# A mixed attention and soft-MoE kernel on one core: the first v load on another queue, and phi loaded in long rows

## The chip, the cores and the metric

One core of a Trainium2 chip runs the whole program. The metric is the device time of one execution in microseconds. Five engines work side by side: TensorE (PE in the profile, its weight loads as PEld), VectorE (DVE), ScalarE (ACT), GpSimd (POOL) and SyncE (SP). Each runs its own instructions in order and waits on semaphores for the others. Transfers are issued from an engine's queue and run on the core's 16 DMA engines.

## The reference, cut to what matters

The input is q, k, v (4 batches, 8 heads, 768 positions, 64 features, float32), a flag per head, and the MoE's phi (512 x 32), w1 (8 x 512 x 1024) and w2 (8 x 1024 x 512), all float32.

```
scores = q @ k.T / 8                       # per batch and head
keep   = causal                            # flagged heads
keep   = causal & (first 4 keys | the last 64 keys)   # the other heads
x      = softmax(scores where keep) @ v    # as (3072, 512): position by (head, feature)

logits = x @ phi                           # (3072, 32)
d      = softmax over the 3072 rows of logits
slots  = d.T @ x                           # 32 slots, 4 for each of 8 experts
slot_out[e] = relu(slots[e] @ w1[e]) @ w2[e]
c      = softmax over the 32 slots of logits
out    = c @ slot_out                      # (3072, 512) float32
```

## The kernel before

The work is cut into eight quads Q = 0..7, half a batch each (four heads), and sixteen pairs n of heads, two in a quad. For each quad, q, k and v are loaded as float32 and written to SBUF as bfloat16 by GpSimd's queue, 96 partitions by 2 x 1024, into one of two buffers for each of the three (`raws`, which lie in the memory of w2s[4], w2s[5] and w2s[6]; the masks `msk` lie in w2s[7]). TensorE turns each with 32 small products (`turn`, L120; in the order list Tq0.0, Tk0.0, Tv0.0 and so on), and VectorE or ScalarE copies the result out of PSUM (L130, L132). v is turned back into blocks (L138). Scores are made in units of 512 columns for two heads (`qk`, L166), exponentiated by ScalarE (L174), masked by VectorE (L193), multiplied with v (`pvmm`, L208) and normalised (L222). After each batch the rows of x are turned (L231) and multiplied with phi (L255), exponentiated over slots (L260) and put in output order by GpSimd (L264). After the last batch come the experts: w1 (L639), the turn of the hidden rows (L652), w2 (L666), and then the output products (L704, L720), evacuated by VectorE and ScalarE and stored by SP's queue (L690).

The order of all this on every engine is written out by hand in `ORDER`; each engine executes its part in that order. In it, Y means `zeros`: products of zeros that keep TensorE busy (L422). Eleven of them run at the very front, ahead of Tq0.

All loads of q, k, v and the weights are issued by GpSimd (L103, L391, L394, L397), in the order of `LOADS`. The first six (q0 k0 v0 q1 k1 v1) are issued at once. Each later one is issued, in that order, when the buffer that it goes to has been turned: q2 behind both halves of Tq0, k2 behind Tk0, v2 behind Tv0. The w entries take the weights in turn, w1 of expert 0 first. The last ones, w2 of experts 4 to 7, take the place of the raws and the masks and so come at the end, experts 6 and 7 in two column halves each.

phi is (512, 32). It is wanted in SBUF as 128 partitions by 4 chunks, the rows in the order of the heads in a pair's halves, and repeated four times along the columns. Before, SP's queue issues four loads into `phf`, each of 128 runs of 32 floats, once the second half of Tv1 has been issued:

```
nc.gpsimd.memset(phf[:, 0, 0:1], 0.0)      # L503: makes SP's queue wait for this point
for hp in range(2):
    for qh in range(2):
        nc.sync.dma_start(phf[64 * hp:64 * hp + 64, 2 * qh:2 * qh + 2, :], ...)   # L506
```

and GpSimd casts and repeats it into `phi` behind Tv2 (L510). The first use of phi is at L255, at 41 us. SP's queue issues besides only the head flags `ri` at the front (L409) and the stores at the end.

GpSimd's instructions at the front are, in order: the issue of q0, an iota (L412), the issues of k0, v0, q1, k1, v1, `perm` (L456), and the issues from q2 on, each with its wait. ScalarE's first ones are the load of its table, a one-column exponential, and the first half of kT (L130).

Of the kernel before, what the change touches and what calls it, by code (L numbers as in the profile page):

```python
# [10 lines left out]
F32 = mybir.dt.float32  # L11
# [24 lines left out]

LOADS = "q0 k0 v0 q1 k1 v1 q2 k2 v2 w q3 k3 v3 w q4 k4 v4 w q5 k5 v5 w q6 k6 v6 w q7 k7 v7 w".split()

ORDER = """
Tq0.0 Tq0.1 E eq0.0 eq0.1 Y4 Tk0.1 H2.3 H1.2 Tk0.0 H1.1 ek0.1A H0.1 H0.0 ek0.0 H0.2 H0.3 Y4 Q0.1 H1.3 Q0.4
# [34 lines left out]
class Attn:  # L77
# [19 lines left out]
        self.lg, self.el, self.ep, self.tp = {}, {}, {}, {}  # L97


    def load(self, t, Q):  # L100
        b, h0 = Q // 2, 4 * (Q % 2)
        s = self.src[t][b, h0:h0 + 4].rearrange("(hp hq) (r t) d -> (hq r) hp (t d)", hp=2, t=16)
        self.nc.gpsimd.dma_start(self.raws[t][Q % 2][:96], s)  # L103


    def blocked(self, t, Q):
# [223 lines left out]
def kernel(  # L330
# [13 lines left out]
    nc = tc.nc  # L344
    P = 128
    B, H, S, D = q.shape
    n_sink, window = int(n_sink), int(window)
    ES = moe_phi.shape[1]
# [8 lines left out]
    w2s = [singles.tile([P, 8, DM], BF16, name=f"w2_{e}") for e in range(NE)]  # L357
    raws = {}
    for i, t in enumerate("qkv"):
        w = w2s[4 + i].rearrange("p f (hp c) -> p (f hp c)", hp=2)  # L360
# [3 lines left out]
    ident = singles.tile([P, P], BF16, name="ident")  # L364
    phi = singles.tile([P, 4, P], BF16, name="phi")
# [23 lines left out]
    def w_load(i):  # L389
        if i < NE:  # L390
            nc.gpsimd.dma_start(w1s[i], moe_w1[i].rearrange("(di do) f -> di do f", do=4))  # L391
        else:
            e = i - NE
            nc.gpsimd.dma_start(w2s[e], moe_w2[e].rearrange("(fi fo) d -> fi fo d", fo=8))  # L394

    def w2_half(e, c):
        nc.gpsimd.dma_start(  # L397
            w2s[e][:, :, 256 * c:256 * (c + 1)],
            moe_w2[e].rearrange("(fi fo) d -> fi fo d", fo=8)[:, :, 256 * c:256 * (c + 1)])
# [5 lines left out]
    at = Attn(nc, tc, ctx, sctx, {"q": q, "k": k, "v": v}, env)  # L405


    ir32 = is_retrieval.tensor.reshape([H]).bitcast(I32)
    nc.sync.dma_start(ri, bass.AP(tensor=ir32, offset=0, ap=[[0, P], [1, 2 * H]]))  # L409
    iti = at.small.tile([P, P], I32, tag="iti", bufs=1, name="iti")  # L410
    at.load("q", 0)
    nc.gpsimd.iota(iti, pattern=[[1, P]], base=0, channel_multiplier=-1)  # L412
    for t in ("k0", "v0", "q1", "k1", "v1"):
        at.load(t[0], int(t[1]))

    zw = msk[:, H - 1, :]
    nc.vector.memset(zw, 0.0)
# [2 lines left out]
    def zeros(c):  # L420
        for i in range(c):
            nc.tensor.matmul(zp[:, i % 2, :], zw[:, :128], zw, start=True, stop=True)  # L422

    zeros(11)
    nc.vector.memset(quarter, 0.25)  # L425
    nc.vector.memset(zero, 0.0)
    nc.scalar.activation(colpart[:, 0:1], quarter, ACT.Exp)
# [23 lines left out]
    nc.vector.tensor_copy(fmask[:, :, 0], r0)  # L451


    nc.vector.tensor_scalar(marks[:, 0], r0, -1.0, 1.5, op0=ALU.mult, op1=ALU.add)
    nc.vector.tensor_scalar(marks[:, 1], r1, -1.0, 1.5, op0=ALU.mult, op1=ALU.add)
    nc.gpsimd.tensor_scalar(perm, iti, tkf[:, 2:3], None, op0=ALU.is_equal)  # L456
# [14 lines left out]
    def weights(c):  # L471
        for _ in range(min(c, 12 - wi[0])):
            w_load(wi[0])
            wi[0] += 1

    phf = at.small.tile([P, 4, ES], F32, tag="phf", bufs=1, name="phf")


    unread = []
# [6 lines left out]
        for i in range(c):  # L486
            nc.tensor.matmul(unread[0][:, 1, :448], ident, w1s[0][:, 0, :448], start=True, stop=True)

    queue = LOADS[6:]
    turns = {}  # L490

    def issue():

        while queue:
            x = queue[0]
            if x != "w" and turns.get((x[0], int(x[1]) - 2), 0) < 2:
                return
            queue.pop(0)
            weights(1) if x == "w" else at.load(x[0], int(x[1]))

    def load_phi():

        nc.gpsimd.memset(phf[:, 0, 0:1], 0.0)  # L503
        for hp in range(2):
            for qh in range(2):
                nc.sync.dma_start(phf[64 * hp:64 * hp + 64, 2 * qh:2 * qh + 2, :],  # L506
                                  moe_phi.rearrange("(qh hp a d) s -> qh hp d a s", qh=2, hp=2, a=2)[qh, hp])

    def copy_phi():
        nc.gpsimd.tensor_copy(phi.rearrange("p c (o s) -> p c o s", o=4),  # L510
                              phf.rearrange("p c (o s) -> p c o s", o=1).to_broadcast([P, 4, 4, ES]))

    def after_turn(t, Q):
        turns[t, Q] = turns.get((t, Q), 0) + 1
        issue()
        if (t, Q, turns[t, Q]) == ("v", 1, 2):
            load_phi()
        if (t, Q, turns[t, Q]) == ("v", 2, 2):
            copy_phi()
        if (t, Q, turns[t, Q]) == ("v", NQ - 2, 2):  # L520
            weights(12)
        if (t, Q, turns[t, Q]) == ("v", NQ - 1, 2):
            for e in (4, 5):
                w_load(NE + e)
            w2_half(6, 0)
# [3 lines left out]
    for name in ORDER:  # L529
        op, arg = name[0], name[1:].rstrip("A")  # L530
        eng = "ACT" if name[-1] == "A" else "DVE"
        a = arg.split(".")
# [13 lines left out]
        elif op == "N":  # L546
            at.norm(*[int(x) for x in a])
        elif op == "X":
            at.x_transpose(int(a[0]))
        elif op == "L":  # L550
            at.logits(int(a[0]), [int(c) for c in a[1]])
        elif op == "E":
            expert_masks()
        elif op == "S":
            at.exp_slots(int(arg))
        elif op == "B":
            at.slots_back(int(arg))
        elif op == "D":
            at.dispatch(int(arg))
        elif op == "Z":  # L560
            fill(int(arg))
        elif op == "Y":
            zeros(int(arg))
        elif op == "T":
            t, Q, h = arg[0], int(a[0][1:]), int(a[1])
            if t == "b":
                at.back(Q, h)
            else:
                at.turn(t, Q, h)
                after_turn(t, Q)  # L570
        elif arg[0] in "qkvb":
            t, Q, h = arg[0], int(a[0][1:]), int(a[1])
            (at.blocked_back if t == "b" else at.turned)(*(() if t == "b" else (t,)), Q, h, eng)
        else:
            {"X": at.x_transposed, "l": at.last_exps, "B": at.slots_turned, "D": at.dispatched}[arg[0]](int(arg[1:]))
# [197 lines left out]
```

## Time and profile before

| | |
|---|---|
| median of 3 runs | 152.35 us |
| the runs | 151.85, 152.35, 257.87 us |
| the profiled execution, whole | 152.03 us |
| its span | 150.3 us |
| busy: PE, DVE, ACT, POOL | 124.2, 113.4, 103.8, 35.0 us |
| moved by GpSimd's queue | 26.22 MB, counted as written |
| HBM read | 52.50 MB |

The span runs from the first to the last instruction of the profiled execution; the rest of its time lies around it. The page gives the busy time of each engine, the span in 40 slices of 3.76 us with a digit for the busy share in tenths, the share of the DMA engines and the GB/s that they moved, the chain of waits that ended last, and the costliest groups of instructions by line. A "releaser" is what ended an idle time. A load that changes float32 to bfloat16 is counted with the bytes that it writes.

### The profile page before, as it was taken

The numbers are of one execution on the slowest core, as the hardware profiler recorded it, in microseconds if no ns is written. First come the engines' busy times: TensorE is split into PE (matmuls) and PEld (weight loads), VectorE is DVE, ScalarE is ACT, GpSimd is POOL, SyncE is SP. The second block draws the span as 40 slices with busy tenths as digits, with TensorE's granted clock in tenths as the row PEclk, the third lists the DMA queues.
The fourth block names the chain that finished last, engine by engine and source line by source line (L and its number), as shares of the span: only waits on it lengthen the run. The fifth ranks groups of instructions, "written<-read, shape, count | busy, mean of one in ns | idle before, by whom it ended". The sixth has DMA issues, their size and how long they took to land.

```text
span 150.3 us, 5215 instructions
## 1 busy us (share of the span) xinstructions
PE 124.2 (83%) x2301; PEld 82.5 (55%) x2303; DVE 113.4 (75%) x257; ACT 103.8 (69%) x142; POOL 35.0 (23%) x68
## 2 busy tenths in 40 slices
PE   6799999999999999999999998987989923984000
PEld 2356677677667666658657766554764701651000
DVE  4998999999969999998999998899724301767000
ACT  3059899999899999889989987997054000788000
POOL 6724311411145021335800002800600000000000
PEclk9999999999999999999999999999999995699755
DMA  2999999999999999999999999999999999789995
GB/s 25 202 210 209 210 225 208 209 228 201 211 227 200 217 226 196 226 208 206 219 217 227 216 212 212 214 222 216 216 214 212 192 199 193 174 273 345 342 401 202
DMA packets 16838, 32.91 MB, mean 219 GB/s; under 512 B 1712, under 2 KB 9904, under 8 KB 15024
## 3 DMA queue, kind: packets, MB, share of 16 engines
q0 software_dynamic: 11168, 26.22, 91.0%
q1 hardware_dynamic: 5648, 6.37, 12.4%
q8 instruction: 18, 0.29, 0.7%
q14 instruction: 4, 0.03, 0.1%
HBM read 52.50 MB, written 6.29 MB: 391 GB/s over the span
## 4 chain that ended last, share of the span: by engine, by line
PE 32%; issue 20%; DMA 17%; ACT 13%; POOL 7%; DVE 2%; ACTq 0%; POOLq 0%
DMA w<-in_moe_w_dram 14%; PE sc L166 9%; PE pv L208 7%; ACT pT L174 7%; DMA w<-in_k_dram 4%; ACT ot L710 3%; PE tpv L120 3%; POOL expT L264 3%; PE tpk L120 2%; PE b L704 2%; PE tpx L231 2%; POOL w L394 2%; PE tpb L138 2%; PE lgs L255 1%; PE tpq L120 1%
## 5 line engine op out<-in xcount | busy, mean ns | idle before, releaser
L174 ACT ACTIVATE pT<-sc 128x1024 bf16<-128x1024 f32 (+1 forms) x96 | 81.1, 929 | 5.2 <-PE sc L166 4.9
L193 DVE TENSOR_TENSOR pT<-pT,w 128x1024 bf16<-128x1024 bf16 (+2 forms) x64 | 32.7, 527 | 2.6 <-ACT pT L174 2.5
L166 PE MATMUL sc<-qT,kT 64*128 64x512 bf16 (+3 forms) x256 | 32.5, 309 | 2.0 <-ACT pT L174 1.3
L208 PEld LDWEIGHTS <-pT 128*128 128x128 bf16 x672 | 25.0, 97 | 9.3 <-issue 7.2
L208 PE MATMUL pv<-vb,pT 128*128 128x65 bf16 x352 | 28.3, 194 | 0.1
L208 PE MATMUL pv<-vf,pT 128*128 128x65 bf16 x320 | 24.3, 194 | 0.0
L120 PEld LDWEIGHTS <-w 96*64 96x64 bf16 x768 | 18.6, 109 | 9.3 <-issue 6.2
L222 DVE TENSOR_TENSOR xb<-pv,rs 128x768 bf16<-128x768 f32 (+1 forms) x17 | 15.5, 910 | 0.6
L166 PEld LDWEIGHTS <-kT 64*128 64x128 bf16 x256 | 10.4, 93 | 9.8 <-issue 3.7
L710 ACT ACTIVATE ot<-b,rrow 128x256 f32<-128x256 f32 x16 | 6.3, 482 | 13.5 <-PE b L704 13.5
L264 POOL COPY expT<-ep 128x128 bf16<-128x128 bf16 x18 | 6.8, 426 | 21.8 <-ACT ep L260 21.8
L153 DVE TENSOR_TENSOR vf<-vb,fmask 128x528 bf16<-128x528 bf16 x16 | 11.2, 700 | 0.0
L666 PE MATMUL b<-w,hT 128*32 128x256 bf16 x128 | 5.7, 290 | 5.2 <-DMA w<-in_moe_w_dram 5.2
L103 POOL DMA_DIRECT2D w<-in_k_dram x8 | 5.1, 640 | 18.2 <-PE sc L166 12.0
L236 DVE COPY xT<-tpx 128x768 bf16<-128x768 bf16 x16 | 8.7, 551 | 0.7 <-PE tpx L231 0.7
L120 PE MATMUL tpq<-ident,w 96*64 96x96 bf16 x256 | 8.1, 209 | 0.8 <-DMA w<-in_q_dram 0.8
L231 PE MATMUL tpx<-ident,xb 128*128 128x128 bf16 x96 | 8.0, 218 | 1.0 <-DVE xb L222 0.8
L103 POOL DMA_DIRECT2D w<-in_q_dram x8 | 5.4, 670 | 13.3 <-PE tpq L120 12.4
L120 PE MATMUL tpk<-ident,w 96*64 96x96 bf16 x256 | 8.3, 208 | 0.2 <-DMA w<-in_k_dram 0.2
L120 PE MATMUL tpv<-ident,w 96*64 96x96 bf16 x256 | 8.3, 209 | 0.0
L132 DVE COPY qT<-tpq 128x768 bf16<-128x768 bf16 x15 | 8.0, 550 | 0.3 <-PE tpq L120 0.3
L422 PE MATMUL zp<-w 128*128 128x512 bf16 x21 | 7.0, 459 | 1.3 <-DVE quarter L425 1.2
(108 smaller groups left out, 153.4 us busy)
## 6 DMA issues: line engine op xcount, KB each, us to landing
w<-in_moe_w_dram POOLq DMA_DIRECT2D x14, 1024.0 KB, 18.9
out_dram<-ot SPq DMA_DIRECT2D x16, 256.0 KB, 3.2
w<-in_q_dram POOLq DMA_DIRECT2D x8, 384.0 KB, 12.5
w<-in_k_dram POOLq DMA_DIRECT2D x8, 384.0 KB, 10.9
w<-in_v_dram POOLq DMA_DIRECT2D x8, 384.0 KB, 11.0
w<-in_moe_w_dram POOLq DMA_DIRECT2D x4, 512.0 KB, 23.2
out_dram<-ot SPq DMA_DIRECT2D x4, 512.0 KB, 4.6
phf<-in_moe_phi_dram SPq DMA_DIRECT2D x4, 16.0 KB, 8.9
```

The source lines that it names most:

```text
L103: self.nc.gpsimd.dma_start(self.raws[t][Q % 2][:96], s)
L120: self.nc.tensor.transpose(tp[64 * hp:64 * hp + 64, x, :], raw[:96, hp, s * 64:s * 64 + 64], self.ident[:96, :96])
L153: self.nc.vector.tensor_mul(vf, self.vbs[n // 2 % 2][:, n % 2, :, :4, :], fm.to_broadcast([128, 2, 4, VW]))
L166: nc.tensor.matmul(sc[:, hh, o:o + w], kT[ps, (g0 + j) * 128:(g0 + j + 1) * 128], qT[ps, g0 * 128 + q0:g0 * 128 + q0 + w], start=True, sto ...
L174: self.nc.scalar.activation(self.pT[n][:, :, lo:hi], self.sc.pop((n, u))[:, :, :hi - lo], ACT.Exp, scale=self.scale)
L193: nc.vector.tensor_mul(v, v, m)
L208: self.nc.tensor.matmul(pv[:, i * 65:(i + 1) * 65], pT[:, hh, o:o + 128], (vb if i - j <= 1 else vf)[:, j, :65], start=(j == 0), stop=(j = ...
L222: nc.vector.tensor_mul(x[:, hs], pv[:, :, :, :64], rs[:, :c].to_broadcast([128, c, 6, 64]))
L231: self.nc.tensor.transpose(tp[:, i * 128:(i + 1) * 128], self.xb[b][:, i, n4 * 128:(n4 + 1) * 128], self.ident)
L236: self.nc.vector.tensor_copy(self.xT[n // 4][:, n % 4], self.tp.pop(("x", n, 0)))
L264: self.nc.gpsimd.tensor_copy(self.expT[:, b, t].rearrange("g (p s) -> g p s", s=16), self.ep[b][:, t].rearrange("g (s p) -> g p s", p=8))
L710: nc.scalar.activation(o[:, r, :], op[:, r, :], ACT.Copy, scale=rr[:, r:r + 1])
```

## The change

v0, the first load of v, is taken out of GpSimd's list. ScalarE's queue issues it as the program's first transfer, as float32, into memory that w2 of expert 3 takes later (`stage`). GpSimd casts it into its raw buffer after the issue of v1. phi is loaded by SP's queue right behind the head flags, each partition taking four rows of phi, 512 bytes, in one run. ScalarE casts it, TensorE turns it in four products (one for each of the four rows), ScalarE copies that out, and eight products with the identity put it in the order that the kernel wants; ScalarE copies and repeats it into `phi`. These products stand between the zeros at the front and Tq0: nine zeros, the four, two zeros, the eight. The loads, the memset and GpSimd's cast of before are gone.

```diff
-LOADS = "q0 k0 v0 q1 k1 v1 q2 k2 v2 w ...
+LOADS = "q0 k0 q1 k1 v1 q2 k2 v2 w ...
...
-    def load(self, t, Q):
+    def load(self, t, Q, queue=None, dst=None):
         b, h0 = Q // 2, 4 * (Q % 2)
         s = self.src[t][b, h0:h0 + 4].rearrange("(hp hq) (r t) d -> (hq r) hp (t d)", hp=2, t=16)
-        self.nc.gpsimd.dma_start(self.raws[t][Q % 2][:96], s)
+        d = self.raws[t][Q % 2] if dst is None else dst.rearrange("p (hp c) -> p hp c", hp=2)
+        (queue or self.nc.gpsimd).dma_start(d[:96], s)
...
     ir32 = is_retrieval.tensor.reshape([H]).bitcast(I32)
+    stage = w2s[3].rearrange("p f c -> p (f c)").bitcast(F32)
+    at.load("v", 0, nc.scalar, stage)
     nc.sync.dma_start(ri, bass.AP(tensor=ir32, offset=0, ap=[[0, P], [1, 2 * H]]))
     iti = at.small.tile([P, P], I32, tag="iti", bufs=1, name="iti")
+    phf = w2s[2][:, 0, :2 * 4 * ES].bitcast(F32)
+    nc.sync.dma_start(phf, moe_phi.rearrange("(p j) s -> p (j s)", j=4))
     at.load("q", 0)
     nc.gpsimd.iota(iti, pattern=[[1, P]], base=0, channel_multiplier=-1)
-    for t in ("k0", "v0", "q1", "k1", "v1"):
+    for t in ("k0", "q1", "k1", "v1"):
         at.load(t[0], int(t[1]))
+    nc.gpsimd.tensor_copy(raws["v"][0][:96].rearrange("p hp c -> p (hp c)"), stage[:96])
...
-    zeros(11)
+    zeros(9)
...
+    ph4 = w2s[2][:, 1, :4 * ES]
+    nc.scalar.copy(ph4, phf)
+    phr = at.scp.tile([ES, P, 4], F32, tag="sc", name="phr")
+    for j in range(4):
+        nc.tensor.matmul(phr[:, :, j], ph4[:, ES * j:ES * j + ES], ident, start=True, stop=True)
+    phT = w2s[2][:ES, 2, :]
+    nc.scalar.copy(phT, phr.rearrange("s p j -> s (p j)"))
+    zeros(2)
+    php = at.scp.tile([P, 4, ES], F32, tag="sc", name="php")
+    for n in range(4):
+        for hp in range(2):
+            h = 4 * (n // 2) + n % 2 + 2 * hp
+            nc.tensor.matmul(php[64 * hp:64 * hp + 64, n, :], phT[:, D * h:D * h + D], ident[:ES, :ES],
+                             start=True, stop=True)
+    nc.scalar.copy(phi.rearrange("p c (o s) -> p c o s", o=4),
+                   php.rearrange("p c (o s) -> p c o s", o=1).to_broadcast([P, 4, 4, ES]))
...
-    queue = LOADS[6:]
+    queue = LOADS[5:]
...
-    def load_phi():
-        nc.gpsimd.memset(phf[:, 0, 0:1], 0.0)
-        for hp in range(2):
-            for qh in range(2):
-                nc.sync.dma_start(phf[64 * hp:64 * hp + 64, 2 * qh:2 * qh + 2, :],
-                                  moe_phi.rearrange("(qh hp a d) s -> qh hp d a s", qh=2, hp=2, a=2)[qh, hp])
-    def copy_phi():
-        nc.gpsimd.tensor_copy(phi.rearrange("p c (o s) -> p c o s", o=4),
-                              phf.rearrange("p c (o s) -> p c o s", o=1).to_broadcast([P, 4, 4, ES]))
...
-        if (t, Q, turns[t, Q]) == ("v", 1, 2):
-            load_phi()
-        if (t, Q, turns[t, Q]) == ("v", 2, 2):
-            copy_phi()
```

More of the change, by code (lines that the diff above doesn't have):

```diff
@@ L35, in unit_pieces @@
     return out
-LOADS = "q0 k0 v0 q1 k1 v1 q2 k2 v2 w q3 k3 v3 w q4 k4 v4 w q5 k5 v5 w q6 k6 v6 w q7 k7 v7 w".split()
+LOADS = "q0 k0 q1 k1 v1 q2 k2 v2 w q3 k3 v3 w q4 k4 v4 w q5 k5 v5 w q6 k6 v6 w q7 k7 v7 w".split()
 ORDER = """
@@ L474, in weights @@
             wi[0] += 1
-    phf = at.small.tile([P, 4, ES], F32, tag="phf", bufs=1, name="phf")
     unread = []
```

## The prediction

> **What bounds the kernel now.** I read the page first, for the shape of the run, then the chain that ended last, then busy time by stage at the front and at the end, then the timeline around the waits.
>
> ```profile
> PEclk9999999999999999999999999999999995699755
> DMA  2999999999999999999999999999999999789995
> ...
> q0 software_dynamic: 11168, 26.22, 91.0%
> ```
>
> The DMA row is full from the second slice on: GpSimd's queue carries 26.22 MB (as written; the source is float32, twice that) at some 210 GB/s. The chain says how it ends:
>
> ```profile
> 105.35 20.53 DMA w<-in_moe_w_dram
> 125.88 0.04 issue
> 125.92 1.05 PE b L666 x11
> ```
>
> A w2 half is issued at 105.35 and lands 20.5 us later, behind everything issued before it. The stages show what the engines do meanwhile, and what the first microseconds look like (columns: window and its length, then busy us of PE, PEld, DVE, ACT, POOL, granted clock, DMA share, GB/s):
>
> ```profile
> 1.50:2.00 0.50, 0.50 (x2) 0.15 (x1) 0.00 (x0) 0.50 (x1) 0.50 (x1) 1.00 0.03 4
> 2.00:2.50 0.50, 0.50 (x3) 0.21 (x2) 0.05 (x1) 0.21 (x2) 0.41 (x3) 1.00 0.06 7
> 2.50:3.00 0.50, 0.50 (x3) 0.22 (x2) 0.47 (x5) 0.00 (x0) 0.50 (x1) 1.00 0.71 51
> 3.00:3.50 0.50, 0.50 (x3) 0.15 (x2) 0.43 (x3) 0.00 (x0) 0.50 (x2) 1.00 0.21 33
> 3.50:4.00 0.50, 0.50 (x2) 0.15 (x1) 0.46 (x3) 0.00 (x0) 0.50 (x2) 1.00 1.00 164
> ```
> ```profile
> 120.00:122.00 2.00, 0.59 (x20) 0.31 (x9) 0.00 (x0) 0.00 (x0) 0.00 (x0) 1.00 1.45 201
> 122.00:124.00 2.00, 0.38 (x2) 0.10 (x2) 0.00 (x0) 0.00 (x0) 0.00 (x0) 0.87 1.46 196
> 124.00:126.00 2.00, 0.08 (x4) 0.08 (x7) 0.00 (x0) 0.00 (x0) 0.00 (x0) 0.50 1.45 197
> ```
>
> So the end is set by a transfer stream that starts at 3.5 us and runs without a hole to about 129; all compute that can be done is done at 120.6, 5.3 us before the last first-half weights land. The stream's capacity before 3.5 us is nearly unused. An edit is worth what it does to the stream; a later front of the compute is free up to a point worked out below.
>
> ```profile
> 5.94 0.87 PE L120 MATMUL tpq<-ident,w 96*64 96x96 bf16 x32 [0.83 <-DMA w<-in_q_dram]
> 7.93 0.87 PE L120 MATMUL tpk<-ident,w 96*64 96x96 bf16 x32 [0.15 <-DMA w<-in_k_dram]
> ...
> 55.26 0.63 POOL L103 DMA_DIRECT2D w<-in_k_dram  x1 [8.05 <-PE sc L166]
> ...
> 123.43 0.38 PE L666 MATMUL b<-w,hT 128*32 128x256 bf16 x2 [2.84 <-DMA w<-in_moe_w_dram]
> ```
> ```profile
> w<-in_k_dram POOLq DMA_DIRECT2D x1, 384.0 KB, 6.9
> phf<-in_moe_phi_dram SPq DMA_DIRECT2D x4, 16.0 KB, 8.9
> ri<-in_is_retrieval_dram SPq DMA_DIRECT2D x1, 8.0 KB, 2.5
> ```
>
> **The change, part by part.** The sum is made against the profiled execution, 152.03 us (span 150.3, 1.73 around it); the median shown, 152.35, is 0.3 above it.
>
> *v0 leaves GpSimd's stream.* 393,216 bytes at 210 GB/s are 1.87 us less of it. On ScalarE's queue v0 is 786,432 bytes written as float32. The nearest row is the late float32 stores in 4 KB packets (403 GB/s from 144 to 148): 1.95 us. The issue can leave where SP's ri does, at 0.73, and ri's first packets show at 1.74. Free from there to 4.0, counting the stream's bytes against 210 GB/s, are 0.26+0.48+0.38+0.42+0.11 = 1.65 us, so 0.3 of v0 falls into the stream. Gain 1.87-0.3 = 1.6; lower bound 1.2 if the share column (0.71 at 2.5 to 3.0) is taken as occupied, upper 1.87.
>
> The Trainium skill (DMA: Bandwidth & Descriptors, section "Issuing engines are not separate DMA queues") says that DMAs from whatever engine run on the same 16 engines and interleave, so that a second issuing engine saves issue time only. By that rule moving v0 to another queue is worth nothing in itself; with the rows above it is worth the idle front alone, which is how I count it.
>
> *phi.* Four loads of 128 packets of 128 bytes ran from 23 to 31 us beside the stream; from 26 to 32 the queues together moved 216 GB/s, of which phi was some 11, so the stream had 205 instead of 214: 0.27 us lost over 6 us. Now it is one load of 128 packets of 512 bytes, 64 KB more in the crowded front, 0.15. Net gain 0.1 (0 to 0.27). GpSimd also loses a memset (0.13) and the phi cast (0.61, after 1.7 of waiting at 30 to 31.7); the next issue behind it waited for PE anyway, so nothing.
>
> Gain of the stream, G: 1.6 (1.1 to 2.1).
>
> *GpSimd's queue.* One issue fewer (0.65), so v1's issue ends at 4.9; then the cast of 96x2048, four times the phi cast's 128x512 (0.61): 2.4 us, to 7.3 if v0 has landed by 4.9. Behind it stand perm (0.69) and the issue of q2, which goes at 8.0 instead of 7.12, then k2. Cover: q2 landed 11.1 us after its issue against 4.6 for q0 on an empty stream, so 6.5 us of lateness cost nothing. The cast also has to be done by Tv0, at 10.24: 2.9 us of cover, after which PE would wait.
>
> *phi's chain stands ahead of Tq0 in PE's order.* Copy on ScalarE, four products, copy, eight products, and only then q0's turn. Cost after phi has landed: copy 128x128 about 0.3 (L285's 128x192 takes 0.33), four 128-wide products 0.4 (L295: six in 0.49), copy 32x512 0.69 (L644's 128x512), eight small products 0.3 (L248: 18 in 0.60), four handovers of 0.05: 1.9. The two zeros lie under the second copy, the broadcast copy into phi (0.7) under Tq0, before ScalarE's first kT copy.
> When does phi land? Lower: ri's packets end at about 3.05 and phi's 128 follow on the same queue at ri's pace (1.3 us): 4.3. Upper: the phf row, 7.9 to 9.9 us after issue, from 1.1: 9.0 to 11.0. From 25 to 30 us phi's packets alternated one for one with the stream's, 110 of each a microsecond; with v0 and q0 both in the way, twice that, so 128 take 1.2 to 2.4 us. I take 5.2. Tq0 then starts at 7.1 instead of 5.94. q0 itself, behind the last of v0, lands at about 6.4 and doesn't decide. With 0.2 for DVE beside the cast, the compute front is X = 1.4 us late (0 to 6).
>
> *Where X is paid.* Compute ends at 122.0 instead of 120.6, before the weights (125.9-1.6 = 124.3). But loads are issued when PE has freed a buffer, and the stream now runs 1.6 ahead of issues that come 1.4 later. The thinnest place is k6: issued at 55.26, landed 6.9 us on, against q0's 4.6 on an empty stream: 2.3 us of cover. Summing the stream's packets, the bytes ahead of k6 were moved at 59.6; less q0's 1.5 from issue to first packet the cover is 2.8. A hole of X+G less 2.55 = 0.5 us opens there.
>
> *End.* PE sat idle from 120.6 and its clock was granted at half from 123.5 to 130.3, so L666 took 1.04 us for 14 products (0.61 at 131.2, at full clock) and the 16 of L704 behind it 3.25 (1.91 at 132.4). With compute 1.4 later and weights 1.1 earlier PE waits from 122.0 to 124.8, with two products in between, about too short for that; stores begin a little earlier. 0.3, because the second half of the output waits for the last w2 half at 131.2 whatever PE does. Lower 0, upper 1.1: L666's 0.43 and half of L704's 1.34, the rest of which ScalarE's eight copies (3.3 us) hide.
>
> Sum: 152.03 - 1.6 - 0.3 + 0.5 = **150.6**.
>
> **The rivals.**
>
> *phi lands as late as it did (slower).* Speaking for it: phf's 7.9 to 9.9 us when the engines were full, and v0 fills them now. Against: ri, at the same early time, took 2.5. Landing at 9.0, Tq0 at 10.9, X = 5.0; PE idle from 4.4 to past 9 loses its clock as it did at 123.5, another 1.0. Hole 6.0+1.6-2.55 = 5.05: 152.03-1.6+5.05 = 155.5. It decides from X = 2.6, where hole and gain are equal.
>
> *Everything fits (faster).* v0 wholly in the idle front (1.87), phi's 0.27, no hole, and the 1.1 of a kept clock, with stores filling the 1.7 us in which the DMA engines idle between 128 and 133: 148.8. For it: PE may fall behind by less than 0.7. Against: at 131.2 PE waited for the last w2 half, so a faster first half of the output is only partly worth its time.
>
> *The pipe is the same.* If v0's packets take turns with q0's from the start, 1.95 us replace 1.87: 152.1. Against it, 1.65 us of idle engines. It is the rule of the Trainium skill named above (DMA: Bandwidth & Descriptors, same section) at its strictest.
>
> *The cast stops DVE.* A cast of 2.4 us beside DVE's work from 5 to 7.5 us, masks and qT copies, in the worst case adds all of itself to X: 3.8, hole 2.85, 153.0 with the end's 0.3. Against: beside phi's cast at 31.66 the DVE copy took 0.55 us, its mean. The Trainium skill (SBUF — State Buffer, section "Who interferes with whom") has GpSimd and some DVE modes exclude each other for a whole instruction; that DVE copy read PSUM, so no run here shows the case.
>
> **How the numbers follow.** Forecast 0.42, all fits 0.20, phi late 0.20, same pipe 0.10, cast 0.08. A measurement of this kernel can tell about 2%, 3 us. Below 149.0 lies the second case (0.20), above 155.1 the third (0.20), the rest within. The range leaves out half of the fast and half of the late case, 0.2: 148.8 to 155.5; the forecast's own is 149.6 to 151.6.
>
> **What would show it.** Right: stream share near 1 by 2.5 us; phi landing near 5; Tq0 at 6.5 to 7.5 behind the phi products; the w2 half that L666 waits for landing near 124.8; clock 1.0 between 123 and 130. Wrong: Tq0 past 8.5, a half clock before 12 us, a DMA share clearly under 1 around 55 to 62, or PE waiting for the cast at Tv0. If the weights land no earlier than 125.9 with no hole, the idle front was not room.

## The result

The changed kernel takes 156.56 us (median, 156.13 to 157.29) against 152.1: a ratio of 1.0304, 95% interval 1.0271 to 1.0337. It is slower, where 150.6 us was forecast. (The 152.1 is the median of four runs, one of which, a slow one, took 257.87 us; the ratios here and below leave slow runs out.) The profiled execution took 157.29 us with a span of 155.5, against 152.03 and 150.3 before: 5.2 us of span to explain.

The page of the changed kernel, the rows and the queue that were shown of before (q10 is ScalarE's queue, with v0 on it):

```profile
PEclk9999999999999999999999999999999999599855
DMA  1999999999999999499999999999999999989996
...
q0 software_dynamic: 10960, 25.82, 87.5%
q10 hardware_dynamic: 208, 0.79, 1.9%
```

GpSimd's queue has v0's 0.39 MB less to move, as intended. But the DMA row, full before, has a dip to 4 in its 17th slice (62 to 66 us). The windows show that hole and a thinner stretch at 18, and the front (columns as before: window, its length, busy us of PE, PEld, DVE, ACT, POOL, clock, DMA share, GB/s), and the same two later windows of the kernel before:

```profile
2.50:3.00 0.50, 0.50 (x3) 0.22 (x2) 0.47 (x5) 0.16 (x1) 0.50 (x2) 1.00 0.39 26
3.00:3.50 0.50, 0.50 (x3) 0.16 (x2) 0.43 (x3) 0.00 (x0) 0.50 (x2) 1.00 0.32 45
3.50:4.00 0.50, 0.50 (x2) 0.15 (x1) 0.46 (x3) 0.00 (x0) 0.50 (x2) 1.00 0.44 102
...
18.00:20.00 2.00, 2.00 (x48) 1.23 (x48) 2.00 (x9) 2.00 (x3) 0.53 (x1) 1.00 0.96 146
62.00:64.00 2.00, 2.00 (x40) 1.38 (x38) 2.00 (x4) 2.00 (x4) 0.96 (x2) 1.00 0.25 49
```
```profile
18.00:20.00 2.00, 2.00 (x45) 1.52 (x41) 1.91 (x5) 1.62 (x4) 1.30 (x3) 1.00 1.14 216
62.00:64.00 2.00, 2.00 (x43) 1.30 (x40) 1.97 (x6) 1.68 (x4) 1.27 (x2) 1.00 1.18 236
```

From 3.5 to 4.0 the share was 1.00 at 164 GB/s; now it is 0.44 at 102, and nearly all the bytes are v0's (12 packets of 4 KB; the other 28 are of under 512 bytes, on SP's queue). GpSimd's stream, which began at 2.8, moves its first packet at 6.1. The DMA issues, with KB each and us from issue to landing, show what that did to the four loads of the front:

```profile
w<-in_v_dram ACTq DMA_DIRECT2D x1, 768.0 KB, 8.3
...
w<-in_q_dram POOLq DMA_DIRECT2D x1, 384.0 KB, 9.5
...
w<-in_moe_phi_dram SPq DMA_DIRECT2D x1, 64.0 KB, 8.1
ri<-in_is_retrieval_dram SPq DMA_DIRECT2D x1, 8.0 KB, 5.3
```

ri took 2.5 us before, q0 4.6. The timeline says what came of it:

```profile
9.07 1.88 POOL L420 CAST w<-w 96x2048 bf16<-96x2048 f32 x1 [4.17 <-DMA w<-in_v_dram]
...
9.62 1.04 PE L464 MATMUL phr<-ident,w 128*32 128x128 bf16 x4 [4.42 <-ACT w L461]
...
11.87 1.49 PE L121 MATMUL tpq<-ident,w 96*64 96x96 bf16 x32
...
63.04 0.63 POOL L104 DMA_DIRECT2D w<-in_k_dram  x1 [8.06 <-PE sc L167]
...
132.08 0.67 PE L673 MATMUL b<-w,hT 128*32 128x256 bf16 x14 [2.27 <-DMA w<-in_moe_w_dram]
```

Tq0 starts at 11.87, 5.9 us later than before; its 32 products take 1.49 us instead of 0.87. PE had been idle for 4.4 us ahead of phi's products; in late_front below, where PE is kept busy, Tq0 starts almost as late and takes 0.87. By the attention's last exponential (112.2 instead of 104.4) the lateness is 7.8. k6 is issued at 63.04, 7.8 later too, and the last first-half weights let PE go at 132.08 instead of 125.92.

The best view is not one of the profile's. I summed the packets of GpSimd's queue in order of their times until each load's bytes were through, which tells about when its last byte moved. Before, in us, and then the difference from it (v0, which is off the queue in some, is left out of their sums):

```
load   before   after  v0_only  v0_half   v0_sp  v0_later  phi_only  late_front
q0       5.48   +3.48    +3.26    +0.99   +2.54     +0.14     +0.24       +0.07
q1      11.13   +1.57    +1.36    +0.04   +0.64     -0.52     +0.23       +0.06
q2      16.86   +2.15    +1.30    +0.01   +0.51     +4.61     +0.21       +0.02
v2      20.98   +3.11    +1.89    -0.02   +0.57     +4.67     +0.18       +0.77
k5      50.78   +2.95    +2.14    -0.05   +0.55     +4.63     -0.05       +0.97
q6      59.54   +3.82    +3.73    -0.04   +1.16     +5.24     -0.04       +2.22
k6      61.41   +5.81    +4.00    +0.06   +2.09     +7.74     -0.03       +3.31
w2     123.49   +6.28    +4.49    +0.07   +2.69     +8.33     -0.01       +3.77
last   130.91   +6.11    +4.03    +0.13   +2.33     +7.84     -0.13       +3.10
```

The column "after" has the whole story in four steps. The stream is held 3.48 us at the front. It gets 1.9 back where v0 would have been (between q0 and q1): 1.57 is left. Gaps from 18 to 22 add 1.5, and the hole at k6 adds 3.3 from k5 to the w2 half that PE waits for. Of 6.1 at the last load the span shows 5.2; 0.9 comes back at the end.

### The profile page after: what moved, and what is told of

Read it like the earlier page. It is cut to its first block, busy times and chain, and to the rows that moved or that the text cites. A ratio compares the mean times of both kernels' runs of the same rounds, so it can differ in the third digit from the quotient of the medians.

```text
span 155.5 us, 5235 instructions
## 1 busy us (share of the span) xinstructions
PE 128.0 (82%) x2315; PEld 84.4 (54%) x2315; DVE 113.2 (73%) x257; ACT 105.3 (68%) x145; POOL 35.4 (23%) x66
## 4 chain that ended last, share of the span: by engine, by line
PE 35%; DMA 20%; issue 19%; ACT 10%; POOL 6%; DVE 2%; ACTq 0%; SPq 0%; POOLq 0%
DMA w<-in_moe_w_dram 14%; PE sc L167 9%; PE pv L209 7%; DMA w<-in_moe_phi_dram 5%; ACT pT L175 4%; PE zp L428 3%; PE tpv L121 3%; PE tpq L121 3%; PE tpk L121 3%; POOL expT L265 2%; PE tpx L232 2%; POOL w L395 2%; ACT ot L717 2%; PE tpb L139 2%; POOL w L398 1%
## 5 line engine op out<-in xcount | busy, mean ns | idle before, releaser
L121 PEld LDWEIGHTS <-w 96*64 96x64 bf16 x768 | 19.7, 114 | 8.2 <-issue 7.0
L428 PE MATMUL zp<-w 128*128 128x512 bf16 x23 | 9.5, 544 | 1.2 <-DVE quarter L431 1.2
L121 PE MATMUL tpk<-ident,w 96*64 96x96 bf16 x256 | 8.9, 218 | 0.0
L133 DVE COPY kT<-tpk 128x768 bf16<-128x768 bf16 x14 | 7.6, 550 | 1.7 <-PE tpk L121 1.7
L121 PE MATMUL tpq<-ident,w 96*64 96x96 bf16 x256 | 8.7, 218 | 0.0
L673 PE MATMUL b<-w,hT 128*32 128x256 bf16 x128 | 4.8, 274 | 4.4 <-DMA w<-in_moe_w_dram 4.4
```

Of the source, the lines that this page charges most:

```text
L121: self.nc.tensor.transpose(tp[64 * hp:64 * hp + 64, x, :], raw[:96, hp, s * 64:s * 64 + 64], self.ident[:96, :96])
L133: self.nc.vector.tensor_copy(o, i)
```

## The experiments

Two theories stood after the result. A: v0 on another queue holds GpSimd's stream. B: phi, landing late ahead of Tq0, makes the compute late, and the rest follows from that. Unless a sum says otherwise, times are medians beside the same runs' kernel before, and every kernel computes the whole reference.

**One half each.** v0_only takes phi's new load and products out and loads and casts phi as before:

```
-    phf = w2s[2][:, 0, :2 * 4 * ES].bitcast(F32)
-    nc.sync.dma_start(phf, moe_phi.rearrange("(p j) s -> p (j s)", j=4))
-    ... (the block from ph4 to the copy into phi)
-    zeros(9)
+    zeros(11)
+    ... (load_phi and copy_phi of the kernel before)
```

> The change's first part alone: v0 as float32 by ScalarE's queue and cast by GpSimd; phi in four loads in the middle of the run, as before. Theory A (v0's transfer holds back GpSimd's stream): the stream's first packet comes near 6 us as in the changed kernel, q0 lands near 10.5, Tq0 starts near 10.6, 155 to 156 us. Theory B (phi's chain ahead of Tq0 is what costs): Tq0 starts at 6 to 6.5 and the time is 150.5 to 151.5.

155.79 us, ratio 1.0264 (1.0219 to 1.0308). q0 still lands 9.3 us after its issue and Tq0 waits for it until 10.61. v0 alone makes 3.8 us (beside 152.0) of the changed kernel's 4.5, and the hold of the stream (3.26 at q0) is v0's.

phi_only leaves v0 where it was:

```
-LOADS = "q0 k0 q1 k1 v1 ...
+LOADS = "q0 k0 v0 q1 k1 v1 ...
-    at.load("v", 0, nc.scalar, stage)
-    nc.gpsimd.tensor_copy(raws["v"][0]..., stage[:96])
-    queue = LOADS[5:]
+    queue = LOADS[6:]
```

> The change's second part alone: phi in one load at the front and its products ahead of Tq0; v0 in GpSimd's list as before. Theory A: phi lands near 4.5, as nothing crowds it, Tq0 starts at 6.4 to 7 and the time is 152 to 152.5. Theory B: phi lands at 8 or later, Tq0 starts at 10 or later, 155 us or more.

151.14 us, ratio 0.9959 (0.9936 to 0.9982). In this kernel the same load of phi lands quickly:

```profile
w<-in_moe_phi_dram SPq DMA_DIRECT2D x1, 64.0 KB, 2.6
```

Tq0 starts at 7.13, X is 1.2, and the stream's column stays within 0.3 of before. So phi's load was late in the changed kernel because v0 ran beside it. Theory B falls as a cause of its own. Neither theory's expectation had a gain in it. phi_only's 0.9 us of gain (beside 152.0) comes nearly all at the end, below.

**The products out of the front.** phi_products_late is the full change with phi's cast, rows and order moved ahead of Tq2.1, Tk2.1 and Tv2.1; phi_only_late does the same to phi_only:

```
-    (the block from ph4 to the copy into phi, ahead of the ORDER loop)
+        if name in ("Tq2.1", "Tk2.1", "Tv2.1"):
+            {"Tq2.1": phi_cast, "Tk2.1": phi_rows, "Tv2.1": phi_order}[name]()
```

> The changed kernel with its loads as they are, but phi's cast and products taken out of the front and put ahead of Tq2, Tk2 and Tv2 (eleven zeros at the front again). Theory A: q0 still lands near 10.8, so Tq0 starts near 10.9 instead of 11.9, and the time is 155 to 156. Theory B: Tq0 starts by 7 and the time is 150.5 to 151.5.

157.53 us, 1.04 (1.0329 to 1.0471), above both expectations: no gain at all. Tq0 starts 1 us earlier, at q0's landing (10.90), but the products now interrupt attention, k6 is issued at 64.22 and the last exponential ends at 113.4, each 1.2 later than in the changed kernel.

> phi_only with phi's cast and products taken out of the front and put ahead of Tq2, Tk2 and Tv2. If phi_only's 0.9 us come from the four late loads that are gone, the gain stays: 151 to 151.5. If they come from the compute being a microsecond later, which shortens PE's wait for the last weights and the half clock behind it, the gain changes with the lateness: the products stalled PE by about 2 us in phi_products_late, so compute is late again, with k6's hole opening: 151.5 to 153.

152.93 us, 1.0025 (0.999 to 1.0059), 1.0 more than phi_only by the ratios: the interruption costs the stream 2.6 us from k5 to the w2 half, in a kernel that had no hole there. The front was the better place for them.

**Lateness alone.** late_front is the kernel before with Tq0 held back by idle products:

```
-    zeros(11)
+    zeros(33)
```

> The kernel before with 51 products of zeros at the front instead of 11, so that Tq0 starts near 13.9 and the first exponential near 17.9, as in the changed kernel, with the transfers of before. If a late front is paid through holes in the stream: one of about 1.5 us behind the first six loads (q2 issued near 14.9), one of about 3.5 at the third load before the last of k (k6), and 156 to 157 us. If the loss of the changed kernel lies in the late start of its stream and compute has 5 us to spare, as the wait at the end suggests: 152 to 153.

The expectation was written for 51 such products; the kernel that ran has 33. Its Tq0 starts at 11.12, and k6 is issued 5.4 us late. It took 154.05 us, 1.0142 (1.0106 to 1.0179). By k5 its stream is already 0.97 late; from there its column shows 2.3 to k6 and 2.8 to the w2 half. late_front_w is the same with a weight load taken ahead of k6, so that GpSimd has something to issue before PE frees k6's buffer:

```
-... w q6 k6 v6 w q7 ...
+... w q6 w k6 v6 q7 ...
```

> late_front with one entry of the order of loads moved: the weight load behind v6 goes ahead of k6, so that 1 MB (5 us) stands in the stream while k6's buffer is waited for. If the holes in the stream are how a late front is paid, the hole near 61 to 64 us goes, the last weights land 3 us earlier than in late_front (128 to 129 instead of 132.6 in the sum of bytes) and the time is 151.5 to 152.5, though compute is as late as before (last exponential at 109.8). If lateness is paid otherwise: 154, no change.

152.67 us, 1.0011 (0.9976 to 1.0046): the hole at k6 is gone and most of the loss with it, though Tq0 starts as late (11.20) and the last exponential still ends at 109.45, 5 us late. One window of each, late_front first:

```profile
60.00:62.00 2.00, 2.00 (x50) 1.47 (x48) 2.00 (x5) 2.00 (x5) 1.33 (x3) 1.00 0.32 59
```
```profile
60.00:62.00 2.00, 2.00 (x44) 1.47 (x44) 1.73 (x5) 2.00 (x4) 1.27 (x2) 1.00 1.19 236
```

Share 0.32 against 1.19. But the last weights came less early than expected. The 14 products that wait for a w2 half start at 127.50, against 129.01 in late_front and 125.92 in the kernel before: 1.5 us of the 3 expected, in part because in this execution the stream was already 1.8 late at k5. In its profiled execution, 0.7 slower than that of before, 0.9 us then comes back behind the last weights, as in the changed kernel. So 5 us of lateness of the compute cost little here by itself; most of what late_front lost came through the hole in the stream. after_w makes the same move in the changed kernel:

> The changed kernel with the same entry moved. Its lag has three parts: 1.5 us at the front, 1.4 us of holes behind the first loads, 3 us at k6. Only the last should go: 153 to 154 us, against 156.6. If the front's lag is all that counts, no change.

155.69 us, 1.0196 (1.0138 to 1.0253), above the expected 153 to 154. The dip is gone from its DMA row and its profiled execution is 2.5 us faster than the changed kernel's, and the products that wait for the w2 half start at 129.92 instead of 132.08, but the move is worth 0.9 by the medians and 1.6 by the ratios. So what the k6 hole costs at the end stays open between these; the 3.3 us of the column is what the stream lost by it.

**Where the hold comes from.** v0_sp is v0_only with v0 on SP's queue, behind ri:

```
-    at.load("v", 0, nc.scalar, stage)
     nc.sync.dma_start(ri, ...)
+    at.load("v", 0, nc.sync, stage)
```

> v0_only with v0's load issued by SP's queue behind the head flags instead of ScalarE's queue. If the slow start of v0 and the wait of GpSimd's stream come from the two hardware queues running together: v0 at full pace, landing by 6, the stream's first packets by 4, Tq0 at 6.5 to 8, 151 to 152.5. If any float32 load of this size at the front holds the stream back: first stream packets at 5.5 to 6.5, Tq0 near 10.5, 155 to 156.

154.09 us, 1.0117 (1.0057 to 1.0177). v0 lands 6.1 us after its issue instead of 8.3, ri is back at 2.6, and Tq0 starts at 8.84; the stream still waits, until 5.6, and q0 is 2.54 late. The time lies between the two that were expected. v0_act_alone keeps v0 on ScalarE's queue and puts ri behind it there:

```
-    nc.sync.dma_start(ri, ...)
+    nc.scalar.dma_start(ri, ...)
```

> v0_only with the head flags issued on ScalarE's queue behind v0 instead of SP's, so that only one hardware queue runs at the front. If two hardware queues at once are what made v0 slower on ScalarE's queue than on SP's (8.3 against 6.1 us to landing): v0 now lands about 6 us after its issue, q0 is done 2 to 2.5 us late instead of 3.3, 153.5 to 154.5. If ScalarE's queue itself is slow, or the cold start of the transfer: 8 us again and 155.5 to 156.5. The flags come behind v0, near 7, and hold VectorE's masks, not q0.

154.87 us, 1.0191 (1.016 to 1.0223). Its issue of v0:

```profile
w<-in_v_dram ACTq DMA_DIRECT2D x1, 768.0 KB, 4.9
```

4.9 us against 8.3: the same load from the same queue had been slowed by 8 KB of ri in 64-byte rows on SP's queue at the same time. Without them v0's first packets take 0.17 to 0.24 us each, from 1.76 on, where v0_only's took 0.42 to 1.06, and from 2.5 on it runs at full share:

```profile
2.50:3.00 0.50, 0.50 (x3) 0.22 (x2) 0.47 (x5) 0.49 (x2) 0.50 (x1) 1.00 1.04 352
3.00:3.50 0.50, 0.50 (x3) 0.16 (x2) 0.43 (x3) 0.14 (x1) 0.50 (x2) 1.00 1.00 344
```

So the first microseconds aren't slow in themselves. But even here the stream waits for v0: v0's last packet ends at 5.09 and GpSimd's first one starts at 5.16. ri, now behind v0, lands 5.5 us after its issue and q0 7.9, so most of the loss remains. v0_half sends half of v0 by SP's queue, cast by GpSimd afterwards, and the other half, cast on the way, by GpSimd's queue as before:

```
-    at.load("v", 0, nc.sync, stage)
+    nc.sync.dma_start(stage[:96, :1024], vsrc[:, 0])
...
+    nc.gpsimd.dma_start(raws["v"][0][:96, 1], vsrc[:, 1])
```

> v0_sp with only the first half of v0 as float32 by SP's queue; the other half is cast on GpSimd's queue behind k0. If the stream waits as long as v0's bytes take: first stream packets near 4.5, q0 done about 1.2 us late instead of 2.5, q1 late by 0.3 to 0.6, time 152 to 153. If it waits for a fixed start-up of the front load: first packets at 5.5 again, q0 2.5 us late, q1 1.5 us late, 154 or more.

152.85 us, 1.0052 (1.0029 to 1.0075). Here the stream starts at 4.1, q0 is held 0.99, and removing half of v0 gives 0.95 back: from q1 on the column is within 0.13 of before. For the stream, half the transfer buys what it costs. The profiled execution, 151.91, is no slower than that of before (152.03); why the median is 0.8 above the same runs' 152.02 the trace does not show.

Its cast runs at 5.5 us, while VectorE still works on the masks. One VectorE instruction takes until the cast ends; v0_half's rows first, then the same instruction in the kernel before:

```profile
5.49 1.03 POOL L422 CAST w<-w 96x1024 bf16<-96x1024 f32 x1
```
```profile
5.54 1.01 DVE L459 CAST fmask<-r 128x8 bf16<-128x8 f32 x1
```
```profile
5.58 0.18 DVE L451 CAST fmask<-r 128x8 bf16<-128x8 f32 x1
```

The two end at 6.52 and 6.55. v0_act_alone shows the same: its cast runs from 5.67 to 7.55, and a VectorE instruction of 0.17 us takes 0.96, to 7.58.

v0_later lets the stream start first; a VectorE memset delays v0's issue to 4.8:

```
-    at.load("v", 0, nc.scalar, stage)
+    nc.vector.memset(stage[:, 0:1], 0.0)
+    at.load("v", 0, nc.scalar, stage)    # behind kept's computation
```

> v0_only with v0's load on ScalarE's queue held until a memset on VectorE at about 4.8 us, when GpSimd's stream runs. If the queue that is busy first keeps the engines: q0 lands at 5.9 as before and Tq0 starts near 6, v0's packets begin late (7 to 9 us) and then take turns with the stream's one for one, v0 lands at 12 to 14, and the cast then holds up Tv0 and the issue of q2: 152.5 to 155. If v0's packets have priority whenever they come, q0 or k0 lands 2 to 4 us late: 155 to 156.

159.65 us, 1.0468 (1.0414 to 1.0522), well above the 152.5 to 155 expected. q0 is on time (+0.14). v0's first packet moves 3.5 us after its issue, at 8.3, and then the two queues move about as many packets each; from 8.5 to 10.0:

```profile
q0 software_dynamic: 75, 0.14, 51.2%
...
q10 hardware_dynamic: 72, 0.29, 54.3%
```

v0 lands ten us after its issue, the cast ends at 16.8, and everything behind the cast is late:

```profile
16.86 1.49 PE L121 MATMUL tpv<-ident,w 96*64 96x96 bf16 x32 [5.44 <-POOL w L450]
```

q2's issue, queued behind the cast, moves from 7.12 to 17.37, the stream runs dry from 16 to 18.5 (+4.6 at q2), and k6 adds 3. So v0's place is bad either way: first, it holds the stream; later, its cast holds q2.

**The end.** tail_warm adds to the kernel before twelve products that nobody reads, ahead of the last weights, and phi_only_warm adds them to phi_only:

```
+    wp = bank(HP[5], [P, 512])
+    for i in range(12):
+        nc.tensor.matmul(wp[:, :448], ident, w1s[0][:, 0, :448], start=True, stop=True)
     second((6, 7), (0,), last=True)
```

> The kernel before with the same twelve products. If the half clock is what phi_only's gain came from: 150.8 to 151.5 against 152.1, like phi_only. If not: 152.

151.47 us, 0.9961 (0.9944 to 0.9979). In its profile the half clock still fell, from 125.5, and L666 still took 1.04 us, so how it gains 0.6 us is not shown.

> phi_only with twelve products of no use (448 columns, 2.3 us) between the w2 products of experts 4 and 5 and those of 6 and 7, so that PE doesn't wait for over 2.5 us in one piece. If the half clock behind the wait costs time at the end: the clock stays at 1.0 from 123 to 130, 150.2 to 150.9, against 151.1 for phi_only. If the end goes by the last weights alone: 151.1.

150.92 us, 0.9931 (0.991 to 0.9952): it is faster than both kernels, by 1.1 us than the kernel before beside it (152.02). Against phi_only (151.14) the intervals overlap. Here the products do what they were put in for:

```profile
125.97 0.61 PE L670 MATMUL b<-w,hT 128*32 128x256 bf16 x14 [1.06 <-DMA w<-in_moe_w_dram]
```

0.61 us where before had 1.04, and the sixteen of L708 behind them 1.91 where before had 3.25 (L704). But the half clock comes later, in the next wait, from 131.3 on: L670's second 14 products take 1.04 there. Most of what is won in the one half is paid in the other.

## Why the prediction was wrong

**The step that failed** is "Free from there to 4.0, counting the stream's bytes against 210 GB/s, are 0.26+0.48+0.38+0.42+0.11 = 1.65 us, so 0.3 of v0 falls into the stream." Idle time of the DMA engines was counted as room that v0 could fill while the stream began on time. It isn't: the stream moves nothing until most of v0 has moved. When its first packet starts, 0.63 of v0's 0.79 MB have been started in the changed kernel, 0.33 of the half's 0.39 in v0_half, and all of it in v0_act_alone. This is not for want of free engines alone, since from 3.0 to 4.0 their share in the changed kernel is 0.32 and 0.44; why GpSimd's queue waits even so, no run shows. Measured at q1, the net is a loss of 1.57 (1.36 for v0 alone) in place of a gain of 1.6, with the hold at 3.48 and the return at 1.9, close to the 1.87 that the prediction had. What was mis-sized is the hold, taken at 0.3; v0 in 1.95 us at the rate of the late stores was too fast by far (its packets run from 2.2 to 8.3 in the changed kernel, and from 1.8 to 5.1 in v0_act_alone). v0_half fits the same account with other numbers.

The prediction drew on the Trainium skill (DMA: Bandwidth & Descriptors, section "Issuing engines are not separate DMA queues"), by which DMAs of all engines interleave. v0_later agrees with it, 72 packets to 75. The front does not show it: from v0's first packet at 2.2 to the stream's at 6.1 there was nothing to see of the stream in the changed kernel. The rival built on that rule, "the pipe is the same", was the nearest in kind, but at 152.1 it too was too low: being first cost more than being in the middle.

**phi's landing.** Taken at 5.2, measured 9.27; the upper price of the rival, 9.0, was right, and that rival's total, 155.5, is the nearest to what came. That phi is late because of v0 was right too. But phi isn't what makes Tq0 late: phi alone lands at 3.8, and v0_only, with no phi in the front, has Tq0 at 10.61, waiting for q0. That the total comes so near is luck. Of the 5.9 us at Tq0, phi's chain made 1.3 (11.87 less 10.61). The chain itself took 2.6 us instead of 1.9, mainly because PE ran slowly (phr's four products 1.04, estimated 0.4). The wait is not needed for that: in phi_only the same four follow the zeros at once and take 1.03. phi's net gain for the stream, taken at 0.1, was nil: phi_only is 0.24 late at q0, has won that back by k5, and is 0.01 early at the w2 half.

**The cast** took 1.88 us (estimated 2.4), but began at 9.07, when v0 had landed, not at 4.9. "6.5 us of lateness cost nothing" for q2 was too generous: q2 was issued 6.55 later, at 13.67, on a stream that no longer had v0 ahead of it, and the gaps from 18 to 22 cost 1.5. In the changed kernel q2 waited for Tq0, and not for the cast, which was over at 10.95. In v0_later it waited for the cast, and that cost 4.6 at q2. The rival in which the cast stops VectorE has its mechanism shown, in v0_half and v0_act_alone; in the changed kernel VectorE has nothing to do while the cast runs, so it costs nothing there.

**X and the hole.** X was forecast at 1.4 and is 5.9 at Tq0, 7.8 at k6. The formula, X + G - 2.55, holds in kind, and comes out low: with X = 7.8 and the 2.95 us by which the stream is late at k5 it gives 2.3, and the column shows 2.9 to k6 and 3.3 to the w2 half; for late_front (5.4 and 0.97) it gives 1.9, against 2.3 and 2.8. late_front_w shows that the hole is the main way in which lateness is paid. Its price at the end is less certain (after_w).

**The end.** 0.3 was taken, with 1.1 as the bound; it gave 0.9. phi_only has as much: its last weights move 0.13 earlier and its span is 1.1 shorter. In both the half clock lasted half as long as before, 3.4 us instead of 6.8. What sets that is open. A shorter wait of PE isn't enough: in tail_warm PE waits 0.34 and 2.20 us, less than in the kernel before (2.84 and 2.11), and the half clock lasts 6.8 us all the same.

## What to carry to other kernels

An idle stretch ahead of a full transfer stream is not free room: before a load goes there on another queue, look at which queue has its first packet in first, and expect the stream to start only when most of that load has moved, at the pace that the load has beside whatever else runs then. Then follow the delay to the loads that wait for a buffer: lateness of the compute costs little until GpSimd has nothing left to issue, and the place where that happens first can be moved by the order of the loads. Test the halves of such a change alone; here one half was worth 0.9 us and the other cost 3.8.

## What the runs showed of the hardware

- In the first microseconds of a program a 768 KB load on a hardware queue kept GpSimd's queue out: the stream's first packet came at 6.1 (ScalarE's queue beside SP's), 5.6 (SP's), 5.2 (ScalarE's with SP's idle) or 4.1 (half the bytes), against 2.8. Where the stream ran first (v0_later), both queues moved, 75 packets against 72, and the newcomer's first packet came 3.5 us after its issue.
- Where ri's 64-byte rows came just ahead or beside, the first packets of v0 were slow: 0.9 to 1.4 us for the first eight in v0_sp, against 0.16 to 0.33 from 4 us on. In v0_act_alone, with ri behind v0, they took 0.17 to 0.24 from the start, at 1.76. GpSimd's first packets in the kernel before, while ri was under way, took 0.35 to 0.75. The rows alone don't explain it: in v0_act_alone, where ri is under way at 5.2, GpSimd's first six took 0.17 to 0.29.
- Two hardware queues at once cost far more than their bytes: with 8 KB of 64-byte rows on SP's queue beside it, v0 on ScalarE's queue took 8.3 us (v0_only), and without them 4.9; ri itself took 5.3 in the changed kernel instead of 2.5.
- A VectorE instruction of 0.18 us took 1.01 beside a GpSimd cast and ended with it, 0.03 us later (v0_half).
- The clock row shows 1.00 at the front of the changed kernel, though the same 32 products took 1.49 us there and 0.87 before: the trace's first record of the clock is at 16.45. Ahead of that, durations tell more than the row.
- GpSimd casts 96x2048 from float32 to bf16 in 1.88 us, 0.92 ns an element of a partition.
